# Second LayerNorm as a row of factors on the first MLP layer's result, two chunks kept in DRAM, fused GELU steps, and splits of w1 moved within the front

## The chip, the cores and the metric

One Trainium2 chip; the kernel uses one of its cores. The metric is device time in microseconds (us) of one execution. The time before is 902.04 us, the median of 3 runs (901.98 to 902.82).

Five engines run their own instruction streams in order and wait for each other on semaphores: TensorE (PE; weight loads, PEld, overlap its matmuls), VectorE (DVE), ScalarE (ACT), GpSimd (POOL) and SyncE (SP), which here only issues DMAs. DMAs that SP issues are taken in that order, and an issue whose data are not there yet holds every later issue on SP.

## The reference

```python
x  = A_x                                   # 1 x 2048 x 448, float32
xn = layernorm(x)                          # no gain or bias, eps 1e-5
# A: attention, 16 heads of 28, one shared k and v
q = xn @ wq;  k = xn @ wk;  v = xn @ wv
A = softmax(q k^T * 28**-0.5) v @ wo
# B: MLP with a LayerNorm of its own, 448 -> 1792 -> 448, tanh form of GELU
y = layernorm(xn)
B = gelu(y @ w1 + b1) @ w2 + b2
out = x + A + B
```

The second LayerNorm works on rows that are already normalised: their mean is zero, so it only scales each token by one factor 1/sqrt(var + eps).

## The kernel before, in words

The 2048 tokens are 16 tiles of 128 rows and 4 chunks of 512 tokens (c = 0 to 3). Each float32 matmul operand is split in two fp32r parts, high and low ("xh", "xl"; "w1h", "w1l"), and a product is made of high times high, high times low and low times high. One chunk's first-layer or projection result thus takes 11 matmuls of 512 columns (lines 177, 180, 182 of the helper `proj_steps`), here called a slot.

**Front** (0 to 66.4 us). `norm_parts` makes a chunk's turned rows: `center` writes (x - mean) * scale to an "xn" tile (ACT line 260, DVE line 261), `turn` transposes it with four PE transpositions (line 269) into a PSUM tile "m", and ACT line 270 and DVE line 271 split that in "xh" and "xl". Two buffers each hold "xh" and "xl", so two chunks are there at a time. For each chunk 16 / 4 = 4 slots (c, i) of `q_slot` project q, k and v; ACT (line 359) and DVE (line 366) carry the result to "qe", and SP stores it to DRAM "qd" (line 373). Between them the front splits w1: `w1_split` is one ACT copy (line 325) and two POOL subtractions (lines 326, 327), and `w1_load` queues the next load (lines 94 to 96). `norm_both` computes the second LayerNorm's scales "lnq", one number for each of the 2048 tokens, in slots (2,2) and (2,3). In slots (3,0) to (3,2) `norm_parts` runs a second time, on chunk 0, with those scales, since the MLP starts with chunk 0. `b1_turn` (PE line 417) turns the bias of the first layer.

**MLP** (66.4 to 352.3 us). 56 slots (c, ft): 4 chunks by 14 blocks of 128 hidden units. Slot n computes the first layer of its block into PSUM "ph" (11 matmuls; `mlp1`), and then the second layer of slot n-3 (`LAG`), 12 matmuls of 448 columns (`mlp2`, lines 609, 612, 615), between which jobs called `stages` are written: `closing` and `middle` of the GELU, in odd slots of the first chunk the split of a piece of w2 (`high`, ACT line 339; `low`, DVE line 342), and in chunks 0 to 2 the stages of `norm_gen`, which makes the next chunk's second-LayerNorm rows from x lines loaded again (`line`). GELU of a slot takes ACT Square, ACT Identity, DVE `tensor_scalar`, DVE `tensor_mul`, [middle] ACT Tanh, DVE `tensor_scalar`, DVE `tensor_mul`, and [closing, one slot later] ACT Copy to "hh" and DVE subtraction to "hl". "ph" has one PSUM bank of its own; slots 1 and 2 take a bank of the shared ring `mtile` (3 banks). It is free again when ACT line 584 has read it. "hx" and "hz" have two buffers each, "hh" and "hl" four. In slots (3,5), (3,6) and later the MLP also holds first jobs of the attention (`max_job`: DVE lines 519, 520; `load_max`: DVE line 503).

**Attention** (352.3 to 899.8 us): scores, exponentials, products, output. The diff does not touch it.

The order of the instructions on each engine is the order in which the Python code writes them; the generators `slot`, `mlp1` and `mlp2` give control back after each matmul.

## Time and profile before

| what | value |
|---|---|
| median of 3 runs | 902.04 us |
| the profiled execution | 901.57 us, span 899.8 us |
| TensorE clock granted | 1.00 in every stage |
| PE busy | 889.1 us, 99% of the span |
| ACT, DVE, POOL busy | 712.4, 517.7, 68.4 us |
| front | 0 to 66.4 us |
| MLP | 66.4 to 352.3 us |
| attention | 352.3 to 899.8 us |
| DMA moved | 53.99 MB |

The span runs from the first to the last instruction; 1.8 us of the execution lie around it. In the profile's rows, L177 is line 177 of the kernel before; "x11" counts instructions; "out<-in" names the tiles, and the last bracket of a row is how long the engine stood idle before it and what released it. Rows of windows give, for a stretch of the span, the busy us of PE, PEld, DVE, ACT and POOL with the number of instructions, the granted clock, the share of the DMA engines and GB/s.

### The profile page before, as it was taken

How to read it: one execution, taken by the hardware profiler on the slowest of the kernel's cores; microseconds unless marked ns; L12 is line 12 of the kernel's file. 1: busy time of each engine (PE TensorE's matmuls, PEld its weight loads, DVE VectorE, ACT ScalarE, POOL GpSimd, SP SyncE). 2: the span in 40 equal slices, each digit the busy share in tenths (PEclk: the TensorE clock that was granted, in tenths of full speed). 3: DMA queues.
4: the chain of work that ended last, by engine and by line, in shares of the span. 5: the costliest groups of instructions: out<-in, count | busy, mean ns of one | idle time of the engine just before them, and what ended most of it. 6: DMA issues, size and time to landing. Idle time of an engine off the chain costs nothing.

```text
span 899.8 us, 13425 instructions
## 1 busy us (share of the span) xinstructions
PE 889.1 (99%) x4977; PEld 571.0 (63%) x4977; DVE 517.7 (58%) x1064; ACT 712.4 (79%) x1366; POOL 68.4 (8%) x70
## 2 busy tenths in 40 slices
PE   9999999999999999999999999999999999999997
PEld 8778888888888887444444564444564444564445
DVE  7877687576676887654564544564544554545212
ACT  5786664564554456999999969999969999969993
POOL 5330000000000002040000000000000000000000
PEclk9999999999999999999999999999999999999999
DMA  9673122002102014031102211002211002211001
GB/s 303 207 217 122 62 62 82 21 21 70 32 22 62 21 43 122 3 78 43 25 18 61 65 42 42 19 25 55 71 41 43 18 25 53 73 42 39 6 1 43
DMA packets 36265, 53.99 MB, mean 60 GB/s; under 512 B 7766, under 2 KB 24852, under 8 KB 36196
## 3 DMA queue, kind: packets, MB, share of 16 engines
q1 hardware_dynamic: 34788, 52.53, 19.9%
q8 instruction: 40, 0.66, 0.3%
q10 hardware_dynamic: 1408, 0.57, 0.2%
q14 instruction: 29, 0.24, 0.1%
HBM read 37.40 MB, written 14.68 MB: 58 GB/s over the span
## 4 chain that ended last, share of the span: by engine, by line
PE 91%; DVE 3%; ACT 3%; DMA 1%; issue 1%; ACTq 0%; DVEq 0%
PE m L669 27%; PE po L860 25%; PE ph L177 12%; PE m L612 5%; PE m L609 5%; PE m L615 5%; ACT p L670 2%; PE qp L177 2%; PE m L512 2%; PE m L747 1%; PE m L749 1%; PE m L748 1%; PE ph L182 1%; PE ph L180 1%; PE m L269 1%
## 5 line engine op out<-in xcount | busy, mean ns | idle before, releaser
L670 ACT ACTIVATE p<-m 128x512 f32<-128x512 f32 x956 | 490.7, 766 | 30.9 <-PE m L669 30.5
L669 PE MATMUL m<-xh,ks 128*128 128x512 f32 x960 | 272.6, 410 | 0.7 <-DVE tt L519 0.3
L669 PEld LDWEIGHTS m<-xh,ks 128*128 128x128 f32 x960 | 174.3, 187 | 149.4 <-ACT p L670 76.3
L860 PE MATMUL po<-p,vs 128*32 128x512 f32 x2016 | 242.4, 598 | 0.0
L860 PEld LDWEIGHTS po<-p,vs 128*32 128x32 f32 x2016 | 52.6, 109 | 115.9 <-issue 115.9
L583 ACT ACTIVATE hz<-ph,b1s 128x512 f32<-128x512 f32 x54 | 37.2, 688 | 101.2 <-PE ph L182 101.2
L519 DVE STREAM_TRANSPOSE tt<-m 128x512 f32<-128x512 f32 x60 | 43.0, 716 | 110.6 <-PE m L512 110.6
L615 PE MATMUL m<-w2h,hl 128*128 128x448 f32 x224 | 82.8, 370 | 0.0
L612 PE MATMUL m<-w2l,hh 128*128 128x448 f32 x224 | 82.0, 366 | 0.0
L609 PE MATMUL m<-w2h,hh 128*128 128x448 f32 x224 | 81.8, 365 | 0.0
L787 DVE COPY oc<-po 128x512 f32<-128x512 f32 x15 | 10.4, 692 | 103.4 <-PE po L860 103.4
L177 PE MATMUL ph<-xh,w1h 128*128 128x512 f32 x162 | 63.4, 391 | 0.8 <-ACT hx L584 0.8
L177 PE MATMUL ph<-xl,w1h 128*128 128x512 f32 x162 | 63.5, 392 | 0.3 <-DVE xl L271 0.3
L177 PE MATMUL ph<-xh,w1l 128*128 128x512 f32 x162 | 63.4, 391 | 0.0
L802 POOL TENSOR_TENSOR otl<-oc,oth 128x512 fp32r<-128x512 f32 x15 | 23.9, 1591 | 470.4 <-DVE oth L800 244.7
L585 DVE TENSOR_SCALAR hz<-hz 128x512 f32<-128x512 f32 x56 | 25.3, 453 | 55.1 <-ACT hz L583 55.1
L527 ACT ACTIVATE tt<-tt 128x512 f32<-128x512 f32 x60 | 50.8, 846 | 0.0
L533 DVE STREAM_TRANSPOSE p<-tt 128x512 f32<-128x512 f32 x60 | 42.1, 702 | 12.0 <-ACT tt L527 12.0
L589 ACT ACTIVATE hz<-hz 128x512 f32<-128x512 f32 x56 | 35.2, 629 | 14.5 <-DVE hz L586 14.5
L609 PEld LDWEIGHTS m<-w2h,hh 128*128 128x128 f32 x224 | 42.1, 188 | 4.8
L612 PEld LDWEIGHTS m<-w2l,hh 128*128 128x128 f32 x224 | 42.1, 188 | 4.5
L615 PEld LDWEIGHTS m<-w2h,hl 128*128 128x128 f32 x224 | 42.1, 188 | 3.2
(179 smaller groups left out, 1111.7 us busy)
## 6 DMA issues: line engine op xcount, KB each, us to landing
xh<-qd SPq DMA_DIRECT2D x64, 224.0 KB
a<-in_A_x_dram SPq DMA_DIRECT2D x32, 224.0 KB
qd<-qe SPq DMA_DIRECT2D x24, 256.0 KB
ad<-a SPq DMA_DIRECT2D x16, 224.0 KB
a<-ad SPq DMA_DIRECT2D x16, 224.0 KB
raw<-in_B_w_dram SPq DMA_DIRECT2D x7, 448.0 KB
out_dram<-a SPq DMA_DIRECT2D x14, 224.0 KB
raw<-in_B_w_dram SPq DMA_DIRECT2D x4, 336.0 KB
```

The costliest lines, as they stand in the source:

```text
L177: pe.matmul(ps, w, v, start=(n == 0), stop=False)
L519: dve.transpose(tts[u, j], pm)
L527: act.activation(tts[u, j], tts[u, j], AF.Exp, scale=SCALE)
L533: dve.transpose(p0s[u][:, j], tts.pop((u, j)))
L583: act.activation(hz, ph, AF.Square, bias=b1s[:, ft:ft + 1], scale=GELU[0] ** 0.5)
L589: act.activation(hz, hz, AF.Tanh, scale=GELU[1])
L609: pe.matmul(m2[k], hh[:, ts], w2h[:, ft, :], start=(ft == 0), stop=False)
L612: pe.matmul(m2[k], hh[:, ts], w2l[:, ft, :], start=False, stop=False)
L615: pe.matmul(m2[k], hl[:, ts], w2h[:, ft, :], start=False, stop=(ft == NF - 1))
L669: pe.matmul(s, ks[:, kt * P:(kt + 1) * P], qss[u][:, j, :], start=True, stop=True)
L670: act.activation(p, s, AF.Exp, scale=SCALE)
L860: pe.matmul(po[32 * j:32 * j + 32, :], vs[:, kt, :], ps.pop((u, kt, j)), start=(kt == 0), stop=(kt == NT - 1))
```

## The change

- The second LayerNorm's rows are no longer made. `norm_gen` goes, and so does the second pass over chunk 0 in the front. The MLP reads the first LayerNorm's "xh" and "xl", and multiplies the result "ph" by a row of factors, one for each token. `norm_both` transposes "lnq" on PE (L236 of the new code), copies it to "rows", and stores it to DRAM "second" (L239); `load_factors` loads a chunk's 512 factors from there to all 128 partitions (L249), in an "xn" tile.
- Only two chunks fit in "xh" and "xl". The MLP works in the order 2, 3, 0, 1 (`MLP_ORDER`): 2 and 3 are still there after the front. Chunks 0 and 1 are stored to DRAM "xd" (L444, 1 MiB for each of "xh" and "xl") in slots (0,0) and (1,2), and loaded again (L693) at the starts of the MLP's second and third chunk.
- GELU: DVE multiplies "ph" by the factors into "hx" (L591), `closing` of the slot before follows (ACT L604, DVE L606), then ACT Square and Identity on "hx" in SBUF (L593, L594), one DVE `scalar_tensor_tensor` (L595), and in `middle` Tanh (L598) and one more (L599). The factor 0.5 has gone into `closing`. "ph" is now freed by DVE L591. Slot 3 takes its "ph" from the shared ring as well.
- The splits of w1 are written in slots (1,1), (1,3), (2,1), (2,3) and (3,0) to (3,3), and within a slot behind `center` and `turn`; the first loads of w1 are issued in slot (0,1) and no longer at the program's start.

```diff
@@ -28,6 +28,7 @@
 HEAD = P
 LIMIT = 1e30
 LAG = 3
+MLP_ORDER = (2, 3, 0, 1)
 ENGINES = [mybir.EngineType.PE, mybir.EngineType.Activation, mybir.EngineType.DVE, mybir.EngineType.SP]
 ORDER = "YnsMssnsXsossseP"
 SHARES = (8, 8, 8, 7, 7, 7, 7, 8)
@@ -232,10 +232,21 @@
         next(r)
         yield
         next(r)
-        dve.tensor_mul(lnq, lnq, lnr)
-        dve.scalar_tensor_tensor(lnqb, lnp[:, :, 0], -1.0, lnq, op0=ALU.mult, op1=ALU.mult)
+        turned = mtile([NT, P])
+        pe.transpose(turned, lnq, ident)
+        rows = wp.tile([NT, P], F32, name="rows")
+        dve.tensor_copy(rows, turned)
+        nc.sync.dma_start(second, rows)
         act.activation(warm, one, AF.Tanh)
         yield
+
+    second = dram.tile([NT, P], F32, name="second")
+    xd = [[dram.tile([P, 4, CW], F32, name=f"xd{c}{i}") for i in range(2)] for c in range(2)]
+    factors = {}
+
+    def load_factors(c):
+        factors[c] = tmp.tile([P, CW], F32, name="xn", bufs=2)
+        nc.sync.dma_start(factors[c], second[CT * c:CT * c + CT, :].rearrange("k p -> (k p)")[None, :].to_broadcast([P, CW]))
 
     lines = {}
 
@@ -243,10 +254,10 @@
         lines[t] = keep.tile([P, D], F32, name="a", bufs=4)
         nc.sync.dma_start(lines[t], xv[:, t, :])
 
-    def norm_parts(c, second, first=False, bank=mtile):
+    def norm_parts(c, first=False, bank=mtile):
         xh = xt_p.tile([P, 4, CW], F32R, name="xh")
         xl = xl_p.tile([P, 4, CW], F32R, name="xl")
-        xts[c, second] = xh, xl
+        xts[c] = xh, xl
         xns = {}
 
         def center(k):
@@ -255,8 +266,7 @@
                 xn = f(wqp.tile([P, 2, CW], F32R, name="qe", bufs=5))[:, 0, :]
             else:
                 xn = tmp.tile([P, 4 * P], F32, name="xn", bufs=2)
-            scale, bias = (lnq, lnqb) if second else (lnr, lnb)
-            src = lines.pop(t) if second and c else xin[t]
+            scale, bias, src = lnr, lnb, xin[t]
             act.activation(xn[:, 0:D], src, AF.Identity, bias=bias[:, t:t + 1], scale=scale[:, t:t + 1])
             dve.tensor_scalar(xn[:, D:512], src[:, 384:448], scale[:, t:t + 1], bias[:, t:t + 1],
                               op0=ALU.mult, op1=ALU.add)
@@ -273,7 +283,7 @@
         return center, turn
 
     def norm_first(bank):
-        center, turn = norm_parts(0, False, True, bank)
+        center, turn = norm_parts(0, True, bank)
         ends = [bn_end(0, 0, 2), bn_end(0, 2, 2)]
         bn(0)
         bn(1)
@@ -297,16 +307,6 @@
         turn(3)
         next(first)
 
-    def norm_gen(c, bank):
-        center, turn = norm_parts(c, True, False, bank)
-        for k in range(CT + 1):
-            if k > 0:
-                turn(k - 1)
-            yield
-            if k < CT:
-                center(k)
-            yield
-
     wl_q = []
 
     def w1_load(s):
@@ -346,7 +346,7 @@
         return high, low
 
     def q_slot(c, i):
-        xh, xl = xts[c, False]
+        xh, xl = xts[c]
         cols = slice(c * CW, (c + 1) * CW)
         ms = slice(i * P, (i + 1) * P)
         ps = qpp.tile([P, CW], F32, name="qp")
@@ -383,9 +383,6 @@
 
     act.activation(warm, one, AF.Sqrt)
     first = split_weights()
-    w1_load(0)
-    w1_load(1)
-    w1_load2(2)
 
     def qbank(shape):
         return qpp.tile(shape, F32, name="qp")
@@ -425,8 +422,10 @@
     qss, ots = {}, {}
 
     evac, vt = None, None
+    w1_turns = ((1, 1), (1, 3), (2, 1), (2, 3), (3, 0), (3, 1), (3, 2), (3, 3))
     for c in range(NCH):
-        center, turn = norm_parts((c + 1) % NCH, c + 1 == NCH)
+        if c + 1 < NCH:
+            center, turn = norm_parts(c + 1)
         for i in range(4):
             ev = q_slot(c, i)
             if vt is not None:
@@ -435,8 +434,22 @@
             if evac is not None:
                 vt = evac()
             evac = ev
-            if i in ((2, 3) if c == 0 else (1, 3)):
-                n = 2 * c + i // 3
+            for job in more.get((c, i, True), ()):
+                job()
+            for part, k in (("", "c0 c1", "t0 c2 t1 c3", "t2 t3") if c == 0 else
+                            ("c0 c1", "t0 c2 t1 c3", "t2 t3", ""))[i].split() if c + 1 < NCH else ():
+                (center if part == "c" else turn)(int(k))
+            if (c, i) in ((0, 0), (1, 2)):
+                for k in range(2):
+                    nc.sync.dma_start(xd[c][k], f(xts[c][k]))
+            if (c, i) == (0, 1):
+                w1_load(0)
+                w1_load(1)
+                w1_load2(2)
+            if (c, i) in ((3, 0), (3, 1)):
+                load_factors(MLP_ORDER[i])
+            if (c, i) in w1_turns:
+                n = w1_turns.index((c, i))
                 w1_split(n)
                 if n < 2:
                     w1_load(n + 4)
@@ -444,11 +457,6 @@
                     w1_load2(6)
                 elif n in (4, 5):
                     w2_load(n - 4)
-            for job in more.get((c, i, True), ()):
-                job()
-            for part, k in (("", "c0 c1", "t0 c2 t1 c3", "t2 t3") if c == 0 else
-                            ("c0 c1", "t0 c2 t1 c3", "t2 t3", ""))[i].split():
-                (center if part == "c" else turn)(int(k))
             for job in more.get((c, i, False), ()):
                 job()
     evac()
@@ -573,29 +581,29 @@
     def split(c, ft):
         return c == 0 and ft % 2 == 1
 
-    def mlp1(c, ft):
-        yh, yl = xts[c, True]
-        ph = mtile([P, CW]) if c == 0 and 0 < ft < LAG else php.tile([P, CW], F32, name="ph")
+    def mlp1(c, ft, closing):
+        yh, yl = xts[MLP_ORDER[c]]
+        ph = mtile([P, CW]) if c == 0 and 0 < ft <= LAG else php.tile([P, CW], F32, name="ph")
         fs = slice(ft * P, (ft + 1) * P)
         yield from proj_steps(ph, lambda b: w1h[:, b, fs], lambda b: w1l[:, b, fs], yh, yl)
         hx = hrp.tile([P, CW], F32, name="hx", bufs=2)
         hz = hrp.tile([P, CW], F32, name="hz", bufs=2)
-        act.activation(hz, ph, AF.Square, bias=b1s[:, ft:ft + 1], scale=GELU[0] ** 0.5)
-        act.activation(hx, ph, AF.Identity, bias=b1t[:, ft:ft + 1])
-        dve.tensor_scalar(hz, hz, 1.0, 1.0, op0=ALU.mult, op1=ALU.add)
-        dve.tensor_mul(hz, hz, hx)
+        dve.tensor_mul(hx, ph, factors[MLP_ORDER[c]])
+        closing()
+        act.activation(hz, hx, AF.Square, bias=b1s[:, ft:ft + 1], scale=GELU[0] ** 0.5)
+        act.activation(hx, hx, AF.Identity, bias=b1t[:, ft:ft + 1])
+        dve.scalar_tensor_tensor(hz, hz, 1.0, hx, op0=ALU.add, op1=ALU.mult)
 
         def middle():
             act.activation(hz, hz, AF.Tanh, scale=GELU[1])
-            dve.tensor_scalar(hz, hz, 0.5, 0.5, op0=ALU.mult, op1=ALU.add)
-            dve.tensor_mul(hx, hx, hz)
+            dve.scalar_tensor_tensor(hx, hz, 1.0, hx, op0=ALU.add, op1=ALU.mult)
 
         def ending():
             hh = hrp.tile([P, CW], F32R, name="hh")
             hl = hrp.tile([P, CW], F32R, name="hl")
-            act.activation(hh, hx, AF.Copy)
+            act.activation(hh, hx, AF.Copy, scale=0.5)
             hs[c, ft] = (hh, hl)
-            dve.tensor_sub(hl, hx, f(hh))
+            dve.scalar_tensor_tensor(hl, hx, 0.5, f(hh), op0=ALU.mult, op1=ALU.subtract)
 
         return middle, ending
 
@@ -614,7 +622,7 @@
             yield
             pe.matmul(m2[k], hl[:, ts], w2h[:, ft, :], start=False, stop=(ft == NF - 1))
             if ft == NF - 1:
-                t = CT * c + k
+                t = CT * MLP_ORDER[c] + k
                 a = lines.pop(t)
                 dve.tensor_add(a, a, m2[k])
                 nc.sync.dma_start(ad[:, t, :], a)
@@ -628,14 +636,9 @@
         if n < len(mslots):
             if split(*mslots[n]):
                 high, low = w2_split(n // 2)
-            middle, ending = yield from mlp1(*mslots[n])
-        stages = {1: closing, 5: middle}
-        if high is not none:
-            stages = {0: closing, 1: high, 3: low, 5: middle}
-        if n in norms:
-            stages = {4: norms[n], 5: closing, 8: norms[n], 9: middle}
-            if high is not none:
-                stages.update({6: high, 10: low})
+            middle, ending = yield from mlp1(*mslots[n], closing)
+            closing = none
+        stages = {1: closing, 5: middle} if high is none else {1: high, 3: low, 5: middle}
         if n >= LAG:
             yield from mlp2(*mslots[n - LAG], [stages.get(i, none) for i in range(12)])
         else:
@@ -670,25 +673,25 @@
         act.activation(p, s, AF.Exp, scale=SCALE)
         ps[u, kt, j] = p
 
-    norms, ending = {}, none
+    ending = none
     mslots = [(c, ft) for c in range(NCH) for ft in range(NF)]
-    for c in range(1, NCH):
-        g = norm_gen(c, mtile)
-        for i in range(CT + 1):
-            norms[NF * (c - 1) + 5 + 2 * i] = lambda g=g: next(g, None)
     firsts = {(NCH - 1, 9 + j): {12: f"s{j}", 16: f"x{j}", 20: f"b{j}"} for j in range(4)}
     for n in range(len(mslots) + LAG):
         c, ft = mslots[n] if n < len(mslots) else (NCH, n - len(mslots))
-        if 3 <= ft < 11 and ft % 2 and c < NCH - 1:
-            line(CT * (c + 1) + (ft - 3) // 2)
         if 9 < ft:
-            line(CT * c + ft - 10)
+            line(CT * MLP_ORDER[c] + ft - 10)
             if ft > 10:
-                a = lines[CT * c + ft - 11]
+                a = lines[CT * MLP_ORDER[c] + ft - 11]
                 dve.tensor_add(a, a, b2b)
         if ft == 0 and n:
-            a = lines[CT * c - 1]
+            a = lines[CT * MLP_ORDER[c - 1] + CT - 1]
             dve.tensor_add(a, a, b2b)
+        if ft == 0 and 0 < c < NCH - 1:
+            later_c = MLP_ORDER[c + 1]
+            xts[later_c] = xt_p.tile([P, 4, CW], F32R, name="xh"), xl_p.tile([P, 4, CW], F32R, name="xl")
+            for k in range(2):
+                nc.sync.dma_start(f(xts[later_c][k]), xd[later_c][k])
+            load_factors(later_c)
         if (c, ft) == (NCH - 1, 2):
             load_q(0)
         if (c, ft) == (NCH - 1, 8):
```

On DVE, in the second slot of the MLP (the first with a split of w2; "m" is its "ph" out of the shared ring, "xn" holds the factors), there stands before:

```order
L591 TENSOR_TENSOR hx<-hx,hz 128x512
L585 TENSOR_SCALAR hz<-hz 128x512
L586 TENSOR_TENSOR hz<-hz,hx 128x512
L598 TENSOR_TENSOR hl<-hx,hh 128x512
L342 TENSOR_TENSOR w2l<-raw,w2h 128x896
L590 TENSOR_SCALAR hz<-hz 128x512
```

and now:

```order
L599 SCALAR_TENSOR_TENSOR hx<-hz,hx 128x512
L591 TENSOR_TENSOR hx<-m,xn 128x512
L606 SCALAR_TENSOR_TENSOR hl<-hx,hh 128x512
L595 SCALAR_TENSOR_TENSOR hz<-hz,hx 128x512
L342 TENSOR_TENSOR w2l<-raw,w2h 128x896
```

The read of "ph" has moved from ACT to DVE, and there it stands behind the last GELU step of the slot before.

On ACT, in the same slot, there stands now:

```order
L604 ACTIVATE hh<-hx 128x512
L593 ACTIVATE hz<-hx,b1s 128x512
L594 ACTIVATE hx<-hx,b1t 128x512
L339 ACTIVATE w2h<-raw 128x896
L598 ACTIVATE hz<-hz 128x512
```

Before, Square and Identity (L583, L584) stood ahead of `closing`; now `closing` is first.

On SP, around slots (1,1) and (1,2) of the front ("ks" and "qd" are k and q, "raw" is a piece of w1), there stands before:

```order
L370 DMA ks<-kl 28x512 x2
L370 DMA ks<-ks 28x512
L373 DMA qd_69<-qe 64x512
L373 DMA qd_70<-qe 64x512
L373 DMA qd_69<-qe 128x512
L373 DMA qd_70<-qe 128x512
```

and now:

```order
L370 DMA ks<-kl 28x512 x2
L370 DMA ks<-ks 28x512
L373 DMA qd_69<-qe 64x512
L373 DMA qd_70<-qe 64x512
L94 DMA raw<-in_B_w_dram 128x3x224
L95 DMA raw<-in_B_w_dram 64x224
L96 DMA raw<-in_B_w_dram 64x224
L373 DMA qd_69<-qe 128x512
L373 DMA qd_70<-qe 128x512
L444 DMA xd_155<-xh 128x2048
L444 DMA xd_156<-xl 128x2048
```

The load of w1 and the two stores of chunk 1's rows have come in between.

On PE, between the last matmuls of slot (2,3) and the first of slot (3,0):

```order
 L180 MATMUL qp<-xh,wah 128x512
 L182 MATMUL qp<-xl,wah 128x512
+L236 MATMUL m<-ident,lnq 16x128
 L177 MATMUL qp<-xh,wah 128x512
 L177 MATMUL qp<-xl,wah 128x512
```

The transposition of "lnq" stands ahead of slot (3,0)'s matmuls.

More of the change, by code (lines that the diff above doesn't have):

```diff
@@ L71, in block_kernel @@
     lnb = wp.tile([P, NT], F32, name="lnb")
-    lnqb = wp.tile([P, NT], F32, name="lnqb")
     b1t = wp.tile([P, NF], F32, name="b1t")
@@ L706, in block_kernel @@
                 score(0, *early.pop(0))
-    assert not early
     assert not early
```

## The prediction

> **What bounds the kernel now.** I read the busy shares first, then the chain that ended last, then windows by stage, then single slots on PE.
>
> ```profile
> PE 889.1 (99%) x4977; PEld 571.0 (63%) x4977; DVE 517.7 (58%) x1064; ACT 712.4 (79%) x1366; POOL 68.4 (8%) x70
> PE 91%; DVE 3%; ACT 3%; DMA 1%; issue 1%; ACTq 0%; DVEq 0%
> ```
>
> PE is busy for 99% of the span and holds 91% of the chain. A matmul that goes is therefore a gain, and a new wait on PE a loss, of its full length. The windows show where (us; then busy PE, PEld, DVE, ACT, POOL; clock, DMA share, GB/s).
>
> ```profile
> 0.00:66.40 66.40, 62.76 (x360) 53.02 (x361) 50.20 (x139) 48.10 (x82) 27.71 (x42) 1.00 0.78 241
> 66.40:79.80 13.40, 12.56 (x58) 10.32 (x56) 9.39 (x17) 9.23 (x16) 2.05 (x2) 1.00 0.51 178
> 79.80:352.30 272.50, 272.20 (x1288) 237.41 (x1289) 196.15 (x353) 150.45 (x249) 3.62 (x2) 1.00 0.16 47
> 352.30:899.80 547.50, 541.55 (x3275) 270.29 (x3274) 261.99 (x557) 504.60 (x1020) 34.98 (x25) 1.00 0.15 41
> ```
>
> The MLP is PE alone (272.2 of 272.5); DVE has 196 of 272, ACT 150, so whole steps saved there pay nothing by themselves. The front leaves PE 3.6 us idle and loads the DMA engines to 0.78. The attention (547.5) keeps its code, and I leave it as it is. The chain shows one MLP slot with and one without transpositions:
>
> ```profile
> 115.58 2.05 PE ph L177 x9
> 120.98 2.09 PE ph L177 x9
> ...
> 284.08 2.05 PE ph L177 x9
> 289.02 2.05 PE ph L177 x9
> ```
>
> 5.40 us with four transpositions, 4.94 without.
>
> **A, transpositions gone from the MLP: -6.4.**
>
> ```profile
> L269 PE MATMUL m<-ident,xn 128*128 128x128 f32 x112 | 16.4, 276 | 1.8 <-DVE xl L271 1.8
> 89.78 0.39 PE L177 MATMUL ph<-xh,w1h 128*128 128x512 f32 x1
> 298.74 0.39 PE L177 MATMUL ph<-xh,w1h 128*128 128x512 f32 x1
> ```
>
> 48 transpositions lie in 12 MLP slots. The two starts span 41 slots: 298.74 - 89.78 = 208.96, against 41 x 4.94 = 202.54, so 6.42 us over. 12 x 0.46 = 5.5 is the transpositions; 0.9 their waits for "xl" (1.8 in the group). I take all of it; bounds -5.5 and -6.8. The ACT and DVE work that goes with them was beside PE and is worth nothing.
>
> **B, 16 transpositions gone from the front: -1.9.**
>
> ```profile
> 53.67 0.39 PE L177 MATMUL qp<-xh,wah 128*128 128x512 f32 x1
> 56.26 0.23 PE L417 MATMUL m<-ident,b1r 14*128 14x14 f32 x1
> 56.42 0.50 PE L177 MATMUL qp<-xh,wah 128*128 128x512 f32 x1
> 59.05 1.04 PE L269 MATMUL m<-ident,xn 128*128 128x128 f32 x8
> 59.84 0.48 PE L177 MATMUL qp<-xh,wah 128*128 128x512 f32 x1
> 63.75 0.47 PE L177 MATMUL qp<-xh,wah 128*128 128x512 f32 x1
> 66.37 0.39 PE L177 MATMUL ph<-xh,w1h 128*128 128x512 f32 x1
> ```
>
> Slot (3,0) takes 56.42 - 53.67 = 2.75 with one small transposition in it, so 2.50 for 11 matmuls. Slot (3,1) takes 3.42: 0.92 for the first eight. The next eight are like them (3.91 in all, with v's turning beside them): 1.0.
>
> **C, PE waits for the factors: +2.5.**
>
> ```profile
> 55.33 0.54 DVE L198 SCALAR_TENSOR_TENSOR lnq<-rs 128x16 f32<-128x16 f32 x1
> ```
>
> The new transposition of "lnq" stands ahead of slot (3,0)'s matmuls, which PE reached at 53.67; "lnq" ends at 55.33 + 0.54 = 55.87. That is 2.2 us of waiting, and 0.25 for the transposition, like b1's. Behind it in PE's queue is all that is left of the front. Bounds +2.0 and +3.5 (DVE and ACT reach "lnq" a little sooner or later). The copy, the store "second" and the loads of factors come behind it, and have until the first multiplication, after 68.9: some 10 us of cover, nothing.
>
> **D, the stores of chunk 1's rows: +1.8.** Two buffers hold "xh" and "xl"; chunk 3's first `turn` overwrites what "xd" is stored from.
>
> ```profile
> 28.56 0.39 SPq L94 DMA_DIRECT2D raw<-in_B_w_dram  x1
> 30.33 1.00 SPq L373 DMA_DIRECT2D qd<-qe  x2
> ...
> 33.65 0.94 ACT L325 ACTIVATE w1h<-pair 128x896 fp32r<-128x896 f32 x1
> 34.72 1.61 POOL L326 TENSOR_TENSOR w1l<-pair,w1h 128x672 fp32r<-128x672 f32 x1 [6.49 <-DMA qd<-qe]
> 36.10 0.74 ACT L260 ACTIVATE xn<-a,lnb,lnr 128x448 f32<-128x448 f32 x1
> 36.41 0.66 POOL L327 TENSOR_TENSOR w1h<-pair,w1h 64x224 fp32r<-64x224 f32 x1
> ...
> 48.77 0.69 DVE L271 TENSOR_TENSOR xl<-m,xh 128x512 fp32r<-128x512 f32 x1
> 28.00:32.00 4.00, 4.00 (x25) 3.28 (x24) 3.03 (x15) 1.68 (x4) 0.23 (x1) 1.00 0.97 292
> 106.50:107.00 0.50, 0.50 (x4) 0.42 (x3) 0.50 (x1) 0.00 (x0) 0.00 (x0) 1.00 1.04 394
> ```
>
> In (1,1) the split of w1 now stands behind the centering at 36.10. That ends 0.94 sooner, at 35.9, since a split ahead of it went; the split's ACT copy ends at 36.8, POOL (1.61 + 0.66) at 39.1. Then three load issues on SP take 30.33 - 28.56 = 1.77, the next qd pair 1.0: the "xd" stores are issued at about 42. About 0.6 MB is still ahead and they are 2.1 MB: 2.7 MB end at 48.9 by the 394 GB/s row (full queue) and 51.2 by the 292 row (front, short packets between). "xl" is wanted at 48.77, so PE loses 0.1 to 2.4 in (2,2) and (2,3). I take 1.8, nearer to the row of the front; bounds 0 and +3. "xd" of chunk 0 goes out from (0,0) on, 20 us ahead of its overwriting.
>
> [...]
>
> **E, the MLP's first slots: +2.3.**
>
> ```profile
> 79.78 0.50 PE L177 MATMUL ph<-xh,w1h 128*128 128x512 f32 x1 [0.84 <-ACT hx L584]
> L271 DVE TENSOR_TENSOR xl<-m,xh 128x512 fp32r<-128x512 f32 x28 | 18.9, 687 | 1.3
> L766 DVE SCALAR_TENSOR_TENSOR sq<-oc 128x512 f32<-128x512 f32 x15 | 10.4, 693 | 0.5
> L589 ACT ACTIVATE hz<-hz 128x512 f32<-128x512 f32 x56 | 35.2, 629 | 14.5 <-DVE hz L586 14.5
> L339 ACT ACTIVATE w2h<-raw 128x896 fp32r<-128x896 f32 x7 | 6.6, 944 | 0.0
> L342 DVE TENSOR_TENSOR w2l<-raw,w2h 128x896 fp32r<-128x896 f32 x7 | 7.6, 1085 | 0.0
> ```
>
> GELU of one slot is now a serial chain: multiplication 0.69, Square 0.63, Identity 0.63, step 0.69, Tanh 0.63, step 0.69 = 3.96, with handoffs about 4.05; where w2 is split (copy 0.94, subtraction 1.09 in the chain's middle) about 4.6. The multiplication of slot n stands on DVE behind the last step of n-1, so the chains don't overlap. In steady state 4.05 or 4.6 lies under 4.94. But the first three slots take PE only 2.5 each: counted from the end of slot 0's matmuls, the multiplication of slot 4 begins at 0.1 + 4.05 + 4.6 + 4.05 + 4.6 = 17.4 and ends at 18.1, while PE wants its bank, for slot 5, at 3 x 2.5 + 2.43 + 2.5 + 2.43 = 14.9: 3.2 us late. Before, 66.37 to 89.78 is 23.41, against 3 x 2.5 + 3 x 4.94 = 22.3: 1.1 late (0.84 of it the row at 79.78). 3.2 - 1.1 = 2.1, and 0.2 for "w2l" of the first slots. Bounds +1.2 and +3.2.
>
> **F, the attention's first jobs on DVE: +0.8.**
>
> ```profile
> 307.94 0.71 DVE L519 STREAM_TRANSPOSE xl<-m 128x512 f32<-128x512 f32 x1
> 308.68 0.69 DVE L520 TENSOR_REDUCE mr<-xl 128x16 f32<-128x512 f32 x1
> 309.54 0.39 PE L177 MATMUL ph<-xh,w1h 128*128 128x512 f32 x1
> ```
>
> In (3,5) and (3,6) four such pairs, 1.4 each, share DVE with the GELU. Before, ACT read "ph" past them; now three pairs (4.2) stand between the DVE read of one "ph" and of the next, with 3.4 of GELU steps in a stretch of 4.94: 2.7 over, against a slack of 2.5 by the slot. That gives 0.2, and the small jobs of `load_max` 0.5 more. Bounds 0 and +1.3.
>
> **At nothing:** the reload of "xd" (4.2 MB over 138 us of MLP, DMA share there 0.16); x lines no longer loaded; the last splits of w1, wanted from the MLP's eighth slot on. Without that cover each would be a wait of PE.
>
> **Sum:** -6.4 - 1.9 + 2.5 + 1.8 + 2.3 + 0.8 = -0.9. The profiled execution took 901.57 (span 899.8), 0.47 under the median: 900.7 against it, 901.1 against the median of 902.04.
>
> **Rivals.** Faster or slower means by over 0.2%, 1.8 us: about what a measurement of this kernel can tell from no change.
>
> *The new waits are short, faster (0.36).* The transpositions' 8.3 us are read off PE's own rows, the four waits are derived. If the full queue's rate holds (D 0.1), "lnq" comes with C at 2.0 and the first slots lose 1.2, the sum is -6.4 - 1.9 + 2.0 + 0.1 + 1.2 + 0.5 = -4.5: 897.5. With half of that difference, 899.3. For it: the 394 GB/s row, and PE rows that stretch little. Against: 0.97 of DMA share at 292 GB/s in the front.
>
> *The DMA queue bounds the front, slower (0.18).*
>
> ```profile
> 0.00:50.00 50.00, 46.72 (x279) 40.08 (x279) 36.87 (x107) 33.46 (x58) 21.97 (x36) 1.00 0.80 254
> ```
>
> Until 50 us the queue has 0.20 x 50 = 10 us free. Four stores of 1.05 MB take 10.6 us at 394 GB/s and 14.4 at 292, and w1's first loads have moved behind two of them. If the queue is full, the front ends 4.4 later by the slow rate, in place of D's 1.8, and idle stretches that nothing can fill add to it: at 4.6 and up, the whole is 903.9 or more, which decides it; with 2 us of such stretches 905.7. For it: 0.97 of share. Against: the stores are long packets, and window 106.50 moved such at 394.
>
> *The GELU chain bounds every slot, slower (inside the same 0.18, at 0.04).* The chain passes six handoffs; at 0.16 more each it takes 5.0 and PE waits about 0.07 in each of 49 slots, 3.4 us: 904.5. The row of the first slots speaks against: the six steps leave 0.9.
>
> **How the numbers follow.** Forecast (0.46): -0.9, within 0.2% of the median. Its own range is 900.3 to 903.8. The faster case ends at 897.5 and 899.3, the slower at 903.9 to 905.7. Leaving about 0.1 out on each side gives 898.4 to 904.6. Faster 0.36, same 0.46, slower 0.18.
>
> **What would show it.** A: slot starts 4.94 apart between the MLP's seventh slot and its 48th. B and C: L236 waits on DVE "lnq" for about 2 us, then slots of 2.5 up to the MLP. D: ACT's or DVE's first write of chunk 3's "xh" or "xl" waits for "xd". The MLP should start at 66.37 + 2.5 + 1.8 - 1.9 = 68.8. E: PE waits on DVE L591 for 3 us in slot 5 or about it; the MLP's seventh slot starts at 94.5. F: waits on L591 near 308 and 318. The MLP should last from 68.8 to 351.4. I am wrong if the waits of C, D and E overlap (the sum counts each in full), or if steady slots wait on L591.

## The result, and the profile after

The changed kernel takes 907.80 us (median of 6 runs, 906.71 to 908.70) against 902.01: a ratio of 1.0061, 95% interval 1.0048 to 1.0074. It is slower by 5.8 us by the medians (5.5 by the ratio), where -0.9 was forecast, and outside the range. The profiled execution took 907.85, span 906.1. The page's first and fourth parts read:

```profile
PE 886.4 (98%) x4914; PEld 566.6 (63%) x4914; DVE 492.6 (54%) x975; ACT 710.4 (78%) x1334; POOL 68.2 (8%) x70
PE 88%; ACT 4%; DVE 3%; DMA 3%; SPq 1%; issue 0%; POOL 0%; ACTq 0%; DVEq 0%; POOLq 0%
```

PE has less to do (889.1 before) and 63 fewer instructions, but holds 88% of the chain, not 91%: DMA and ACT have come in. Read by stage, from the starts of slots on PE, the profiled spans differ like this:

| stretch | before | after | difference |
|---|---|---|---|
| to slot (2,2) | 45.93 | 45.44 | -0.5 |
| slot (2,2) | 5.13 | 8.36 | +3.2 |
| slot (2,3) | 2.61 | 5.05 | +2.4 |
| slots (3,0) to (3,3) | 12.70 | 11.11 | -1.6 |
| MLP, first six slots | 23.41 | 28.40 | +5.0 |
| MLP, next 41 slots | 208.96 | 203.64 | -5.3 |
| MLP, the rest | 53.59 | 55.55 | +2.0 |
| attention and end | 547.47 | 548.55 | +1.1 |

The attention itself is the same to 0.1 us: its last DVE addition ends 5.1 us later than before, as its first matmul starts 5.2 later. The last 1.1 us lie behind that addition, where only the output's stores and the closing waits are left; the spans of the six runs differ by 2 us among themselves, and I do not count these 1.1 us to the change.

**The front.** Slot (2,2) on PE before:

```profile
45.93 0.48 PE L177 MATMUL qp<-xh,wah 128*128 128x512 f32 x1
...
49.60 0.72 PE L269 MATMUL m<-ident,xn 128*128 128x128 f32 x4 [0.54 <-DVE xl L271]
50.68 0.63 PE L269 MATMUL m<-ident,xn 128*128 128x128 f32 x4 [0.36 <-DVE xl L271]
51.06 0.48 PE L177 MATMUL qp<-xh,wah 128*128 128x512 f32 x1
```

Chain, PE's timeline and the windows of the changed kernel (in a row of windows the third number from the end is PE's granted clock):

```profile
43.84 7.11 DMA xd<-xl
...
51.00 0.04 issue
51.04 0.69 DVE xl L281
```

```profile
45.44 0.48 PE L177 MATMUL qp<-xh,wah 128*128 128x512 f32 x1
...
51.88 2.27 PE L279 MATMUL m<-ident,xn 128*128 128x128 f32 x8 [3.31 <-ACT w1h L325]
53.80 0.78 PE L177 MATMUL qp<-xh,wah 128*128 128x512 f32 x1
54.37 0.63 PE L177 MATMUL qp<-xl,wah 128*128 128x512 f32 x1
54.80 0.63 PE L177 MATMUL qp<-xh,wal 128*128 128x512 f32 x1
...
58.83 0.27 PE L236 MATMUL m<-ident,lnq 128*16 128x128 f32 x1 [0.55 <-DVE lnq L198]
58.85 0.47 PE L177 MATMUL qp<-xh,wah 128*128 128x512 f32 x1
59.17 0.39 PE L177 MATMUL qp<-xl,wah 128*128 128x512 f32 x1
```

```profile
50.00:55.00 5.00, 3.06 (x11) 2.39 (x12) 3.89 (x8) 3.73 (x7) 2.27 (x2) 0.56 1.00 317
55.00:60.00 5.00, 4.45 (x15) 3.25 (x15) 4.38 (x12) 4.25 (x7) 2.44 (x3) 0.75 0.84 266
```

The store of chunk 1's "xl" lands at 50.95, so DVE writes chunk 3's first "xl" at 51.04 (48.77 before). PE stands still for 3.31 us; the row names ACT, but the chain shows the store behind it. Then PE is slow: its matmuls step by 0.43 us (54.37 to 54.80), against 0.23 before and after, and the granted clock is 0.56 and 0.75. By the time PE reaches the transposition of "lnq" it waits only 0.55 for it.

**The MLP's start.** Before, the last q stores and the first write of "w2h":

```profile
63.67 5.28 SPq L373 DMA_DIRECT2D qd<-qe  x8
73.54 0.94 ACT L339 ACTIVATE w2h<-raw 128x896 fp32r<-128x896 f32 x1
```

After, SP's timeline, then ACT's, DVE's and PE's:

```profile
60.78 0.53 SPq L239 DMA_DIRECT2D second<-rows  x1
61.41 0.84 SPq L373 DMA_DIRECT2D qd<-qe  x2
65.65 0.32 SPq L249 DMA_DIRECT2D xn<-second  x1
...
71.76 3.99 SPq L373 DMA_DIRECT2D qd<-qe  x6
75.81 3.54 SPq L464 DMA_DIRECT2D km<-ks  x4
```

```profile
81.05 0.95 ACT L339 ACTIVATE w2h<-raw 128x896 fp32r<-128x896 f32 x1 [1.87 <-DMA km<-ks]
```

```profile
72.68 0.69 DVE L591 TENSOR_TENSOR hx<-ph,xn 128x512 f32<-128x512 f32 x1 [1.19 <-PE ph L182]
76.98 0.68 DVE L591 TENSOR_TENSOR hx<-m,xn 128x512 f32<-128x512 f32 x1
83.64 0.68 DVE L591 TENSOR_TENSOR hx<-m,xn 128x512 f32<-128x512 f32 x1
87.87 0.68 DVE L591 TENSOR_TENSOR hx<-m,xn 128x512 f32<-128x512 f32 x1
92.56 0.68 DVE L591 TENSOR_TENSOR hx<-ph,xn 128x512 f32<-128x512 f32 x1
```

```profile
69.96 0.40 PE L177 MATMUL ph<-xh,w1h 128*128 128x512 f32 x1
...
82.05 0.47 PE L617 MATMUL m<-w2h,hh 128*128 128x448 f32 x1 [1.86 <-ACT w2h L339]
83.18 0.47 PE L620 MATMUL m<-w2l,hh 128*128 128x448 f32 x1 [0.65 <-DVE w2l L342]
...
93.30 0.50 PE L177 MATMUL ph<-xh,w1h 128*128 128x512 f32 x1 [2.62 <-DVE hx L591]
...
98.36 0.40 PE L177 MATMUL ph<-xh,w1h 128*128 128x512 f32 x1
```

From 62.25 to 65.65 SP issues nothing: the load of the factors waits for the store "second", 8 KB, 4.9 us after its issue. Behind it stand the front's last q stores, issued up to 75.75 (68.95 before). The first write of "w2h" waits for them, since by the program the MLP's w2 tiles take the memory of the front's "qe": 81.05, 73.54 before. (The row names "km", the last transfer that SP issued behind them. By the trace's semaphores the last q store lands at 80.87, and the last of the "km" transfers at 81.31, when the write of "w2h" has begun.) PE loses 1.86 us to that, 0.65 to "w2l" behind it, and 2.62 to the GELU chain (steps of 4.30, 6.66 with the wait for "w2h" in it, 4.23 and 4.69 between the multiplications).

**Steady slots** start 4.967 us apart (mean of the 41 from 98.36 to 302.00), where before they took 4.94 without transpositions and 4.97 or 5.40 around them. In the last chunk PE waits twice for the multiplication beside the attention's first jobs:

```profile
313.57 0.50 PE L177 MATMUL ph<-xh,w1h 128*128 128x512 f32 x1 [0.49 <-DVE hx L591]
324.33 0.50 PE L177 MATMUL ph<-xh,w1h 128*128 128x512 f32 x1 [0.56 <-DVE hx L591]
```

### The profile page after: what moved, and what is told of

Its sections match the earlier page's. It is cut to its first block, busy times and chain, and to the rows that moved or that the text cites. A ratio compares the mean times of both kernels' runs of the same rounds, so it can differ in the third digit from the quotient of the medians.

```text
span 906.1 us, 13176 instructions
## 1 busy us (share of the span) xinstructions
PE 886.4 (98%) x4914; PEld 566.6 (63%) x4914; DVE 492.6 (54%) x975; ACT 710.4 (78%) x1334; POOL 68.2 (8%) x70
## 4 chain that ended last, share of the span: by engine, by line
PE 88%; ACT 4%; DVE 3%; DMA 3%; SPq 1%; issue 0%; POOL 0%; ACTq 0%; DVEq 0%; POOLq 0%
PE m L672 26%; PE po L862 25%; PE ph L177 11%; PE m L617 5%; PE m L620 5%; PE m L623 5%; ACT p L673 2%; PE m L749 1%; PE m L520 1%; PE m L750 1%; PE m L751 1%; PE qp L177 1%; PE ph L180 1%; PE ph L182 1%; PE m L392 1%; DMA pair<-in_B_w_dram 1%
## 5 line engine op out<-in xcount | busy, mean ns | idle before, releaser
L604 ACT ACTIVATE hh<-hx 128x512 fp32r<-128x512 f32 x56 | 35.4, 632 | 47.6 <-DVE hx L599 43.9
L593 ACT ACTIVATE hz<-hx,b1s 128x512 f32<-128x512 f32 x56 | 40.6, 725 | 35.3 <-DVE hx L591 35.1
L595 DVE SCALAR_TENSOR_TENSOR hz<-hz,hx 128x512 f32<-128x512 f32 x56 | 38.8, 692 | 51.7 <-ACT hx L594 51.7
L598 ACT ACTIVATE hz<-hz 128x512 f32<-128x512 f32 x56 | 35.4, 632 | 36.2 <-DVE hz L595 36.2
L599 DVE SCALAR_TENSOR_TENSOR hx<-hz,hx 128x512 f32<-128x512 f32 x56 | 38.7, 690 | 29.0 <-ACT hz L598 28.6
```

What stands on the lines that cost most here:

```text
L593: act.activation(hz, hx, AF.Square, bias=b1s[:, ft:ft + 1], scale=GELU[0] ** 0.5)
L595: dve.scalar_tensor_tensor(hz, hz, 1.0, hx, op0=ALU.add, op1=ALU.mult)
```

## The experiments

Times are medians beside runs of the kernel before on the same chip. Medians of these kernels rest on 4 to 11 runs that spread by 1 to 5 us, so the steps are read from the traces. The last three columns are times in each run's profiled execution, in us from the span's start: the MLP's first slot, the first write of "w2h", and the MLP's seventh slot. The "first stretch" is the time from that first slot to the seventh.

| run | us | ratio to before (95%) | MLP starts | first w2h | 7th slot |
|---|---|---|---|---|---|
| before | 902.0 | 1 | 66.37 | 73.54 | 89.78 |
| after | 907.80 | 1.0061 (1.0048 to 1.0074) | 69.96 | 81.05 | 98.36 |
| early stores | 906.88 | 1.0056 (1.0039 to 1.0073) | 66.53 | 79.36 | 96.67 |
| w2 early | 909.76 | 1.0078 (1.0061 to 1.0095) | 69.69 | 83.10 | 100.44 |
| GELU overlap | 912.91 | 1.0113 (1.0097 to 1.0130) | 69.79 | 81.29 | 104.02 |
| splits back | 905.11 | 1.0036 (1.0024 to 1.0049) | 69.64 | 80.03 | 97.34 |
| factors later | 907.47 | 1.0058 (1.0042 to 1.0075) | 70.25 | 81.05 | 98.38 |
| stores and factors | 905.99 | 1.0041 (1.0027 to 1.0055) | 66.74 | 78.26 | 95.56 |
| four moves | 904.75 | 1.0029 (1.0018 to 1.0041) | 63.99 | 78.34 | 93.93 |
| ring banks | 905.96 | 1.0043 (1.0031 to 1.0055) | 69.92 | 80.51 | 94.94 |
| PE row and moves | 900.87 | 0.9982 (0.9973 to 0.9991) | 65.89 | 76.99 | 91.39 |
| PE row only | 908.98 | 1.0075 (1.0060 to 1.0090) | 71.39 | 80.52 | 97.82 |
| hl first | 907.80 | 1.0065 (1.0049 to 1.0080) | 70.01 | 81.15 | 98.46 |
| no multiplication | 905.82 | 1.0037 (1.0023 to 1.0050) | 71.95 | 81.71 | 100.97 |
| idle filled, 27 | 909.96 | 1.0088 (1.0071 to 1.0105) | 71.52 | 82.35 | 99.67 |
| unfused | 908.65 | 1.0077 (1.0060 to 1.0094) | 70.89 | 81.44 | 102.38 |
| filled, turn late | 909.63 | 1.0080 (1.0063 to 1.0096) | 69.19 | 82.52 | 99.83 |
| turn late | 908.66 | 1.0073 (1.0056 to 1.0090) | 68.38 | 82.33 | 99.64 |
| idle filled, 14 | 910.35 | 1.0086 (1.0068 to 1.0104) | 71.99 | 81.18 | 100.09 |
| best | 898.28 | 0.9964 (0.9951 to 0.9976) | 65.81 | 74.93 | 89.32 |

**Early stores.**

```diff
-            if (c, i) in ((0, 0), (1, 2)):
+            if (c, i) in ((0, 0), (1, 0)):
```

> Chunk 1's two stores to xd are issued in slot (1,0) instead of (1,2); nothing else differs from the changed kernel. Theory: those stores land at 51.0, two us after chunk 3's rows are wanted; PE idles 3.3 us, and its granted clock then falls (0.56 in 50 to 55 us), so that slot (2,3) takes 5.05 instead of 2.6. With the stores early, that idle time is under 1 us, the clock is 1.00 in all front windows, slots (2,2) and (2,3) take about 5.1 and 2.6, PE then waits about 2 us for lnq, and the MLP starts near 67.0 instead of 69.96: about 904.9 us. Rival (the DMA queue is full anyway, so the stores only push w1's loads or the q stores back): the MLP's start stays within 1 us of 69.96 and the time within 1 us of 907.8.

The MLP starts 3.4 us sooner and the clock is 1.00 up to 65 us, as expected; the time falls by less than the theory said. PE's waits (total us, times, longest) in this run:

```profile
PE m L617 <- ACT w2h L339: 3.6, 1, 3.6
PE m L236 <- DVE lnq L198: 2.3, 1, 2.3
```

The wait for "lnq" that was forecast comes out now, and the wait for "w2h" doubles: it hangs on SP's queue, not on PE. And behind that longer wait of 3.6 us PE is slow again, with a clock of 0.66:

```profile
80.00:85.00 5.00, 3.98 (x11) 3.34 (x12) 3.68 (x5) 2.98 (x6) 0.00 (x0) 0.66 0.30 92
```

**w2 early** (two tiles of "first" for w2's first pieces; `w2_load` in (2,1) and (2,3)).

> The first two loads of w2 get a buffer of their own (the one of the first x rows) and are issued in slots (2,1) and (2,3); nothing else differs from the changed kernel. Theory: in the changed kernel they wait for w1's splits to free their buffers, the first lands at 81.0, and ACT's w2h and PE's first second-layer matmul wait 1.9 us for it. With the loads early that wait is gone, the stretch from the MLP's first slot to its seventh goes from 28.4 to 26.5, and the time is about 905.9. Rival (the serial GELU chain alone sets when slot 5 gets its bank): the stretch stays at 28 or above and the time at 907.8.

A miss, and the useful one: with w2 there in time, w2h came later, 83.10. So it was not w2's load that it waited for. Two more transfers had pushed SP's queue: "second" was usable at 71.1, the last q stores were issued up to 79.7.

**GELU overlap** (in the first four slots `middle` of slot n-1 behind slot n's multiplication, Square and Identity).

> In the MLP's first four slots the Tanh half of a slot's GELU is written behind the next slot's multiplication, Square and Identity, so that two slots' chains overlap; nothing else differs from the changed kernel. Theory: there the chain is serial, 4.3 us a slot and 4.7 with a split of w2, and PE waits 2.6 us for slot 5's bank. Overlapped, ACT and DVE need about 2.8 a slot (3.8 with a split); the wait at slot 5 is gone, the late w2 stays, and the first stretch goes from 28.4 to about 25.8: 905.2 us. Rival (late w2 alone is the cause, and the wait at slot 5 follows from it): the stretch stays at 28.

A miss by its own order: on DVE the last step of n-1 now stood behind the multiplication of n, whose Square it had to wait for; from the second on the multiplications came 5.4 to 7.9 us apart, and PE waited 5.5 us for slot 5's bank.

**Splits back** (w1's loads at the program's start, its splits in the old slots, ahead of `center` and `turn`; w2's loads in (2,1) and (2,3)).

> The loads and splits of w1 and the loads of w2 go back to where the kernel before had them (w1's first loads at the program's start, splits in (0,2), (0,3), (1,1), (1,3), (2,1), (2,3), (3,1), (3,3), ahead of center and turn); the rest is as in the changed kernel. Theory: w2 comes early again (first stretch 26.5), the xd stores of chunk 1 no longer stand behind a w1 load that waits for POOL, so they go out about 1 us sooner and PE idles about 2 us instead of 3.3, short enough for the clock to stay: about 903.5. Rival (the move made room for xd's stores in a full queue): without it x rows, w1 and the stores collide in the first 40 us, slots (0,2) to (1,3) grow by 1 us or more in all, and the time is 907 or above.

2.7 us faster than after by the medians; in the trace the MLP's seventh slot starts 1.0 sooner (97.34 against 98.36), and that execution took 906.88. PE's longest wait in slot (2,2) is 2.2 us, but the clock falls to 0.67 in 50 to 55 all the same (0.994 in the mean of that execution), and the MLP starts 0.3 sooner. The moved splits cost; by how much between 1.0 and 2.7, the runs leave open.

**Factors later; stores and factors.**

```diff
-            if (c, i) in ((3, 0), (3, 1)):
-                load_factors(MLP_ORDER[i])
+            if (c, i) == (3, 1):
+                load_factors(MLP_ORDER[0])
 ...
+        if (c, ft) == (0, 8):
+            load_factors(MLP_ORDER[1])
```

> Only the loads of the factors are moved: chunk 2's row is loaded in slot (3,1), behind the q stores of slot (3,0), and chunk 3's in the MLP's ninth slot. Theory: in the changed kernel the load stands in SP's queue from 62.3 and waits until 65.7 for the store second to land; the q stores behind it then land at 81 instead of 76, and w2h, which takes over their buffers, waits for the last of them (ACT 1.9 us, PE 1.9 us at its first second-layer matmul). With the loads moved, ACT's wait for w2h is gone (w2h at 79 or sooner, set by the GELU chain), the stretch from the MLP's first to its seventh slot goes from 28.4 to about 26.5, and the time is about 905.9. Rival (w2h waits for w2's own load, and SP is limited by the 0.4 to 0.9 us of each issue anyway): w2h stays at 80 or later, 907 or more.

> Chunk 1's stores in (1,0) and the factor loads moved, both together. Theory: the early stores alone brought the MLP's start 3.4 us forward, but 1.7 of it was lost again at w2h, which SP's queue held. With both, the MLP starts near 66.5 and its first stretch is 26.5 instead of 30.1: about 903.2 us. Rival (the GELU chain takes what w2h gives up): first stretch 28 or more, 904.7 or above.

SP no longer stands still, but w2h is no sooner in the first. Its DVE row says why, and ACT's row for w2h has no wait any more:

```profile
74.65 0.69 DVE L591 TENSOR_TENSOR hx<-ph,xn 128x512 f32<-128x512 f32 x1 [2.87 <-DMA xn<-second]
81.05 0.93 ACT L339 ACTIVATE w2h<-raw 128x896 fp32r<-128x896 f32 x1
```

The load, issued at 69.61, lands 5 us later. The row of factors takes 4.9 us into DRAM and 5 us out, and waits either in SP's queue or at the first multiplication. With the stores moved as well the MLP starts at 66.74 and its first stretch is 28.8, not 26.5: the chain took it (PE 2.6 at slot 5), as the rival said.

**Ring banks; four moves.**

```diff
-        ph = mtile([P, CW]) if c == 0 and 0 < ft <= LAG else php.tile([P, CW], F32, name="ph")
+        ph = mtile([P, CW]) if c == 0 and ft > 0 else php.tile([P, CW], F32, name="ph")
```

> Only the PSUM banks change: in the first chunk every ph but the first comes out of the shared ring of three, so that DVE's read of one no longer holds the next slot's matmuls. Theory: PE's wait of 2.6 us at slot 5 goes, while those for w2h and w2l (1.9 and 0.7) stay; the first stretch goes from 28.4 to about 25.5, and the time to about 905.0. Rival (the GELU chain itself is the limit, and PE then waits the same time for hh and hl at the second layer): the stretch stays at 28.

> Early stores, factor loads moved, the transposition of lnq behind slot (3,0)'s matmuls, and in the first chunk every ph but the first out of the shared PSUM ring. Theory: each wait goes: the 2.3 us for lnq (MLP starts near 64.2), w2h and the bank of slot 5 (first stretch about 24.5). Against the changed kernel that is 5.8 + 3.9 = 9.7 us: about 898.1, faster than the kernel before (902.0) by 4. Rival (the steps moved give their waits to the next one in line, as the early stores alone did): the seventh slot still starts at 94 or later, and the time is 903 or more.

The ring alone removes the wait at slot 5 (first stretch 25.0): here the theory of E holds. With all four moves (early stores, factors later, the transposition of "lnq" behind slot (3,0)'s matmuls, ring banks) the MLP starts at 63.99, but PE then stands 5.1 us for w2h, since the factors come at 71.9. Each move hands its gain to the next thing in line.

**PE row only; PE row and moves.** "diag" is the identity with each column scaled by one token's factor, and "ones" a tile of ones, so that one matmul brings the row of factors to all partitions:

```diff
+        wide = mtile([P, CW])
+        pe.matmul(wide, ones, diag.rearrange("p k j -> p (k j)"), start=True, stop=True)
+        factors[c] = tmp.tile([P, CW], F32, name="xn", bufs=2)
+        dve.tensor_copy(factors[c], wide)
```

> Chunk 2's row of factors by PE as above, chunk 3's loaded in the MLP; all else as in the changed kernel. Theory: SP no longer waits 3.4 us for the store second, nor issues the two factor loads in the front; the last q stores land 4 us sooner, w2h goes from 81.0 to 78 or so and then follows the GELU chain, PE's wait at the first second-layer matmul goes, the serial chain still holds slot 5's bank: first stretch 28.4 to about 26.8, 906.2 us. Rival (the row's DRAM trip costs nothing, late xd stores and the chain do): 907.8, w2h at 80 or later.

> Early stores, the transposition of lnq behind slot (3,0)'s matmuls, the ring's banks in the first chunk, and chunk 2's row of factors made without DRAM: DVE scales the identity by lnq, one PE matmul with ones spreads it over the partitions, DVE copies it. (The other chunks' rows still come from DRAM, in the MLP.) Theory: in the run with all four waits mended, the first multiplication stood 3.5 us for the factor load (store 5 us, load 5 us). Without it, the multiplication starts right behind the first slot's matmuls, w2h by 75, the MLP starts near 64.5 and its seventh slot near 89.5 instead of 93.9: about 900.3 us, faster than the kernel before (902.2). Rival (w2h waits for the last q stores, which SP issues one by one up to 72 and which land at 78): seventh slot at 93 or later, 904 or more.

Alone it shortens the first stretch to 26.4, as expected, but slot (3,0) grows by 1.3 us and nothing is won. With the moves the kernel is faster than before by 0.18% (0.09 to 0.27), the first version that is. Its PE still waits 1.9 us for w2h.

**Best** (the same, the second w2 load behind the last q stores and km, and two of the last chunk's "ph" from the ring).

> The run with chunk 2's row by PE and all the moves (900.9), and two more: the second load of w2 is issued behind the last q stores instead of ahead of six of them, and in the last chunk the ph of blocks 6 and 8 come out of the shared ring. Theory: the q stores land 0.46 MB sooner, about 1.2 us, and w2h with them; PE's two waits for the multiplication beside the attention's first jobs (0.48 and 0.56) go: 2 us less, about 898.8 us. Rival (w2h is held by SP's issues, not by bytes): only the ring's banks count, 899.9.

```profile
74.93 0.94 ACT L354 ACTIVATE w2h<-raw 128x896 fp32r<-128x896 f32 x1
```

w2h 2.1 us sooner and without a wait, for one SP issue and 0.46 MB out of the q stores' way; of PE's waits in the last chunk 0.4 of 1.0 is left. 898.28, faster than before by 0.36% (0.24 to 0.49).

**hl first; no multiplication; unfused** ask for the 4.967. The second leaves the factors out and lets ACT read "ph" again; the third does that too, with the old GELU steps.

> In the second layer the three products of a tile are taken in the order low-high, high-low, high-high instead of high-high, high-low, low-high; all else as in the changed kernel. Question: why a steady slot takes 4.967 us now and 4.941 before. Theory: PE's separate wait for ACT (hh) stands on the first second-layer matmul, where the width changes; moved one matmul on, the slot is 4.94 again, and 56 slots give 1.5 us: 906.3. Rival (it is not that wait's place): 4.967 in every slot, 907.8.

> The multiplication of ph by the factors is left out (the row is still made, stored and loaded, but not used): ACT's Square and Identity read ph from PSUM again and free it. Theory: the chain of a GELU is 0.7 shorter and ACT may run ahead of DVE, so PE's waits for slot 5's bank (2.6) and at the attention's first jobs (1.1) go; w2h still waits for the q stores (81.0). First stretch 28.4 to about 26, and if the steady 0.026 us belong to PE's wait on DVE for ph, a slot is 4.94: 902.6 us. Rival (the chain has nothing to do with it, w2h decides): first stretch 28 or more, 906 or more.

> As in the run without the multiplication (the factors are left out), and the GELU steps as the kernel before had them (tensor_scalar and tensor_mul instead of one scalar_tensor_tensor; plain copy and subtraction for hh and hl). Question: the steady slot of 4.967 against 4.941. Theory: DVE's fused steps read two SBUF operands for longer beside PE's reads of xh and xl, and slow its first matmuls; unfused, the slot is 4.94 and the time some 1.5 us under the run without the multiplication (905.8): 904.3. Rival (not the fused steps): 4.967 again.

All three keep 4.97. Neither the order of the products, nor who frees "ph", nor the fused steps explain it. The excess is there in the MLP's very first slot, before any GELU step has run: its 11 matmuls take 2.52 us (69.96 to 72.48) against 2.49 before (66.37 to 68.86), and 2.52 in these three runs too. So it belongs to the first-layer matmuls themselves; what slows them stays open. Without the multiplication PE's two waits beside the attention's first jobs are gone (the nine slot starts from (3,5)'s on span 40.95, after 42.54, before 40.67): F is the multiplication's, 1.6 us. At the MLP's start that run tells little: PE idled 4.3 us in its front.

**Idle filled, 27 and 14.** In a PSUM bank of its own:

```diff
+            if (c, i) == (2, 2):
+                spin(27, ballast)
```

> 27 idle 128x128 matmuls of no use (3.3 us) on PE in slot (2,2), in a PSUM bank of their own, where PE waits for chunk 1's stores; the wait itself stays, all else as in the changed kernel. Theory: the granted clock of 0.56 to 0.75 between 50 and 60 us comes from PE's idle 3.3 us. Kept busy, PE has 1.00 there; the eight transpositions take 1.0 instead of 1.9, the matmuls of slot (2,3) step by 0.23 instead of 0.43, lnq comes about 0.9 sooner (its DVE work waits for those transpositions), PE then waits some 2 us for it, and the MLP starts near 69.1: about 907.0 us. Rival (the clock has another cause): 0.56 again and the MLP at 69.96 or later.

> As the run that filled PE's wait in slot (2,2), but with 14 idle matmuls instead of 27: there each took 0.23 us and not the 0.12 assumed, so that they ran 6.3 us and made the transpositions behind them 2.7 us late. 14 take 3.25 and end where the wait ended. Theory: clock 1.00 from 50 to 60 us, transpositions at 51.9 in 1.0 us, slot (2,3) from 52.9, lnq at 58.0 or so (0.7 sooner than in the changed kernel), and PE waits 2.2 us for it: MLP at 69.2 instead of 69.96, about 907.1 us. So the slow clock costs 0.7 here because the wait for lnq lies behind it. Rival (the slow clock's whole 2.5 us come off): MLP at 67.5, 905.3.

The 27 matmuls ran too long (6.29 us), but they answer the question of the cause: PE kept busy, the windows 50 to 60 have a clock of 1.00, and eight transpositions take 1.0 us.

```profile
48.48 6.29 PE L393 MATMUL ballast<-ident 128*128 128x128 f32 x54
54.61 1.04 PE L280 MATMUL m<-ident,xn 128*128 128x128 f32 x8
```

With 14 the clock is 1.00 there too. Then PE waits for "lnq", and the slow stretch comes behind that wait (0.66 in 60 to 65); slot (3,0) takes 4.40 instead of 2.87:

```profile
59.31 0.27 PE L237 MATMUL m<-ident,lnq 128*16 128x128 f32 x1 [2.77 <-DVE lnq L199]
...
60.47 0.63 PE L178 MATMUL qp<-xl,wah 128*128 128x512 f32 x1
60.89 0.63 PE L178 MATMUL qp<-xh,wal 128*128 128x512 f32 x1
```

So the half clock of that stretch (0.56 and 0.75 in the changed kernel, 1.00 in both filled runs) comes from PE's idle time ahead of it, 3.31 us. In the changed kernel it costs next to nothing of its own at the MLP's start: the DVE steps to "lnq" begin at 55.73 there and at 55.76 with 14 matmuls, at full clock, so what the slow clock takes PE would have waited for "lnq". (The wait of 2.77 is some 0.5 longer than it would have been, since one of these steps took 1.60 us in that run and 0.18 in the changed kernel.)

**Turn late, without and with filling** (the transposition of "lnq" behind slot (3,0)'s matmuls).

> Only the transposition of lnq is moved behind slot (3,0)'s matmuls. Theory: in the changed kernel PE reaches it late itself, since slot (2,3) ran at half clock; the wait for lnq is 0.55, so the MLP starts at 69.3 instead of 69.96, and w2h takes that back: 907.5. Rival (the wait for lnq costs what was forecast, 2.5): MLP at 67.5, 905.5 or less.

> The idle matmuls in slot (2,2), and the transposition of lnq behind slot (3,0)'s matmuls. Theory: with the clock at 1.00 and no wait for lnq, slot (2,3) takes 2.6 and the MLP starts near 66.7 instead of 69.96. w2h still follows the last q stores (79 or later), so that the MLP's seventh slot comes near 96.7 and the time is about 906.2. Against the transposition moved alone this isolates the slow clock: about 2.5 us at the MLP's start. Rival (the clock costs nothing): the MLP starts where it does with the transposition moved alone.

Alone it brings the MLP 1.6 us forward, more than expected (the clock came back sooner in that run: 0.95 in 55 to 60, against 0.75); w2h is no sooner, and the time does not fall. The filled one overshot with its 27 matmuls, so its price for the clock was not got.

## Why the prediction was wrong, step by step

The signs of all six terms were right. Against the forecast they missed by +2.7 (E), +1.4 (D), +1.2 (F), +1.1 (A), +0.3 (B) and -0.1 (C). What failed:

- **"At nothing"**, the part of C on the factors' way through DRAM ("some 10 us of cover, nothing"), is the step that failed first. The cover was counted to the first multiplication, and that far it held: the row at 72.68 waits for PE, not for the load. What the load holds up is SP: 3.4 us, with the q stores behind it, and behind these the first w2h, because the MLP's tiles lie where "qe" lay; PE waits 1.86 us for it. With the row made by PE that wait is gone and the first stretch falls by 2.0 us. SP's queue and that reuse were both to be had from the program; I traced the queue for D and not here. Moving w1's pair and w2's loads into the same slots filled SP further.
- **E**, +2.3, was +5.0. The chain was of the right kind (4.30, 4.23, 4.69 against 4.05 and 4.6; Square and Identity take 0.72 from SBUF, I took 0.63) and the ring of banks removes its wait. The wait of 1.86 at w2h was no term, and w2l behind it took 0.65, where the sum had 0.2.
- **D**, +1.8, was +3.2. The store landed within 0.4 us of my estimate (50.95 against 50.57). But 1.8 was the store's delay alone: PE's waits in the slot grew by 2.4 (3.31 against 0.54 and 0.36), as "xl" came 2.3 later and PE 0.5 sooner, and the transpositions at half clock took 0.8 more (1.92 from 51.88 to 53.80, against 1.46 from 49.60 to 51.06 less the wait of 0.36).
- **C**, +2.5, was +2.4 in its slot, which is luck and not its reason: 0.55 of waiting, the rest slow matmuls. "lnq" was late by D (58.69 against 55.87), so C and D overlap, which the prediction had named as a way to be wrong. With D gone (early stores) the wait is 2.3, as forecast.
- **A**, -6.4, was -5.3: the transpositions and their waits went as counted, but each of the 41 slots takes 0.026 us more. Why is open; it is in the first-layer matmuls.
- **B**, -1.9, was -1.6. **F**, +0.8, was +2.0: two waits of 0.49 and 0.56, and slots of 5.07 behind them.

Of the rivals, the one that the DMA queue bounds the front was nearest; it had the place right and gave it 0.18, but named bytes, where SP's order and the memory's reuse were what counted. A steady wait on the GELU chain does not occur.

The way through DRAM took 4.9 us for the store "second" (8 KB, after) and 5 us for the load (256 KB, factors later), with the DMA engines busy at a share of 1.01 in 60 to 65 (after); the prediction had set nothing for either.

## What to carry to other kernels

Follow a new wait on a DMA queue to everything queued behind it, including buffers whose memory a later stage takes over; cover counted to the first reader is not enough. Where a front is a chain of late things, moving one hands its gain to the next: mend the chain (here four moves and the row by PE together; none was faster than before alone) before judging the idea. And a small row that must reach all partitions soon can be spread by one matmul instead of a store and a load: 1.10 us on PE here (best), with five small DVE steps beside it, against 4.9 and 5 us through DRAM.

## What the runs showed of the hardware

Behind some of PE's waits the granted clock fell, and the step of its 512-column matmuls went from 0.23 to 0.43 us: behind 3.31 us (after, in slot (2,2): 0.56 in 50 to 55, 0.75 in 55 to 60), 2.77 us (idle filled, 14, at 59.31: 0.66 in 60 to 65) and 2.66 us (the same run, at 93.44: 0.43 us from 94.59 to 95.02). Windows that lie wholly in such a slow stretch show half (0.50 in 52 to 57 of after, and in 85 to 90 of filled, turn late, behind 4.09 us).

The length of a wait alone does not decide it. The clock also fell behind 2.18 us (splits back, 0.67 in 50 to 55), and stayed 1.00 behind 2.62 us (after, at 93.30), 2.64 and 2.18 us (idle filled, 27, at 94.60 and 60.37) and 2.3 us (early stores, for "lnq"). What decides it is not shown.

Kernels with such a wait mostly show mean clocks of 0.990 to 0.997 and runs that spread by up to 5.4 us; before has 0.998 to 1.000 and a spread of 2.1.
